# A scan and feed-forward kernel on one core: one of the four sums of g goes from the DMA queue to VectorE, with more descriptor scratch, a margin for late DMAs in the build-time order, and runs of 508 and 504 columns

## The chip, the cores and the metric

The kernel runs on one core of a Trainium2 chip. The metric is the device time of one execution in microseconds (us), the median of three runs; lower is better. One further execution was profiled, and every row of the trace below is from it.

## The reference

For two batches of 6080 tokens and 256 channels, a gated scan runs along the tokens, and its result, seen as 12160 rows, goes through two matrix products with a gate between them.

```python
f = lower_bound + (1 - lower_bound) * sigmoid(f_logit)
h = 0
for t in range(S):                      # S = 6080
    h = f[:, t] * h + (1 - f[:, t]) * x[:, t]
    y[:, t] = h
h = y.reshape(12160, 256) @ w_in        # 256 x 2048
g = h * clip(h + 3, 0, 6) / 6
out = g @ w_out                         # 2048 x 256
```

Everything is float32.

## The kernel before

**Runs.** Tokens lie along the free axis, channels on the 128 partitions. The tokens of both batches are cut into 24 runs of at most 512 columns (`token_runs`): 20 runs of 512 and 4 of 480. A product that must be float32-accurate is made of three matmuls, by splitting each operand into a high and a low part (`split`: a copy on ScalarE makes the high part, a subtraction on VectorE the low part).

**Products.** The first four runs multiply directly (`direct`, `single`, `mm2`). The other 20 runs go in ten pairs, one run of each batch, and their 2x2 block products are made with seven products in place of eight (`seven`), which needs sums of operands. For the first product these sums are made of the scan's result (`prep_pair`, tiles `xt`). For the second product of a pair, six of the sixteen blocks of 128 channels are treated so, in nine of the ten pairs (`chain`); the other ten blocks go directly (`mm2`).

**The chain.** `chain` works on four tiles of gated values, g11, g12, g21 and g22, in place: w11, w12, w21, w22. Each is there twice (index z): once for two blocks side by side, 1024 columns wide (names r4, r5, r6, r7 in the built program), once for one block, 512 wide (r10, r11, r12, r13). It makes seven operands, each split into high (`ghi`) and low (`glo`): b11 = w11; t1 = w11 += w12; t3 = w12 += w22; t2 = w11 += w22; b21 = w21; b22 = w22; t4 = w11 += w21. The four sums, for both z, are eight DMAs that add one SBUF tile to another, issued from GpSimd's queue (POOL, `add_into`, L250). TensorE takes the operands in the order b11, t1, t2, b21, b22, t3, t4, three blocks at a time, between other work.

**Order.** Every instruction is first a `Job` with an engine, a planned cost and the jobs that it needs. `ordered` gives each job a due time, plays the engines forward by the planned costs, and writes the program in that order. On the chip every engine then works strictly in its written order and waits by semaphores. So an instruction that waits holds up all that stand behind it on its engine.

**DMA scratch.** `SCRATCH = 512` is the number of bytes of each SBUF partition that hold the descriptors of DMAs issued from POOL. Loads of x and f and the stores of the output are issued from SP.

**Begin.** The first run is loaded and scanned in two halves. `SHARED` lists by (run, first column) the pieces whose second gate scaling (L377) is given to VectorE, not to ScalarE (L381); (0, 256) is the second half of run 0. While TensorE has nothing to do at the begin, it runs matmuls on zeros (L879), as many as the plan has room for.

Of the kernel before, what the change touches and what calls it, by code (L numbers as in the profile page):

```python
# [19 lines left out]
LAG = 4  # L20
PARTS = ((0, 1), (2,))
GROUP = sum(map(len, PARTS))
FILLS = ((2, 3, 2),) * 3 + ((2, 3, 3),)*5
FILLS_FIRST = ((2, 2, 2),) * 8

SHARED = ((0, 0), (0, 256), (1, 0))
# [81 lines left out]
HOP = {"PE": 230, "ACT": 70, "DVE": 70, "SP": 0, "POOL": 0}  # L108
ISSUE = 480
ISSUE_ADD = 1000  # L110
DIRECT = 4
FT = 1
EARLY_AT = {(2, 1): 7, (1, 0): 6, (2, 0): 5}
SCRATCH = 512
LANDING = 1700
SLOW_START = 6500
BYTES_PER_NS = 390
# [3 lines left out]
def ordered(jobs):  # L121


    for j in jobs:
        for b in j.bufs:
            if b.before is not None:
                j.needs.extend(u for u in b.before.users if u is not j)
    for j in jobs:
        j.needs = list(dict.fromkeys(j.needs))
        j.after = []  # L130
    for j in jobs:
        for n in j.needs:
            n.after.append(j)
    left = {j: len(j.after) for j in jobs}
    stack = [j for j in jobs if not left[j]]
    while stack:
        j = stack.pop()
        late = min((d.due for d in j.after), default=1e9) - HOP[j.engine] - j.cost
        if j.moves:
            late -= LANDING + j.moves / BYTES_PER_NS  # L140
        if j.at is None:
            j.due = late
        for n in j.needs:
            left[n] -= 1
            if not left[n]:
                stack.append(n)

    def early(j):
        return max(0.0, j.due - j.ahead) if j.due < 5e8 else 0.0
    missing = {j: len(j.needs) for j in jobs}  # L150
    ready = {e: [] for e in HOP}
    free = dict.fromkeys(ready, BEGIN)
    bus = 0.0
    number = {j: i for i, j in enumerate(jobs)}
    for j in jobs:
        if not missing[j]:
            ready[j.engine].append((early(j), j))
    order = []
    while any(ready.values()):
        best = None  # L160
        for e, waiting in ready.items():
            if waiting:
                start = max(free[e], min(r for r, _ in waiting))
                if best is None or start < best[0]:
                    best = (start, e)
        start, e = best
        could = [x for x in ready[e] if x[0] <= start]
        pick = min(could, key=lambda x: (x[1].due, number[x[1]]))
        ready[e].remove(pick)
        j = pick[1]  # L170
        j.start = start
        free[e] = end = start + j.cost
        if j.moves:
            bus = max(bus, end)
            slow = min(j.moves / 250, max(0, SLOW_START - bus))
            bus += slow + (j.moves - 250 * slow) / BYTES_PER_NS
            end = bus + LANDING
        j.end = end
        order.append(j)
        for d in j.after:  # L180
            missing[d] -= 1
            if not missing[d]:
                at = max(n.end + (HOP[n.engine] if n.engine != d.engine else 0) for n in d.needs)
                ready[d.engine].append((max(at, early(d)), d))
    assert len(order) == len(jobs)
    return order


def token_runs(B, S):


    runs = []
    full = (S - 1) // BANK - 1
    rest = S - full * BANK
    counts = [BANK] * full + [-(-rest // 2), rest // 2]
    assert counts[-1] == counts[-2] <= BANK
    s = 0
    for n in counts:
        runs.extend((b, s, n) for b in range(B))
        s += n  # L200
    return runs
# [3 lines left out]
def gated_scan_then_ffn(  # L205
# [42 lines left out]
    def add_into(size, out, src, needs, bufs):  # L248

        return job("POOL", ISSUE_ADD, lambda: nc.gpsimd.dma_start(out=out(), in_=src(), accum_op=ALU.add),  # L250
                   needs, bufs, moves=2 * size)

    r_ft = Ring(work, "ft", FT, [P, KD, BANK], F32)
    r_xt = Ring(work, "xt", 2, [P, KD, BANK], F32)
    r_xhi = Ring(work, "xhi", 4, [P, KD, BANK], F32R)
    r_xlo = Ring(work, "xlo", 4, [P, KD, BANK], F32R)
    r_bhi = Ring(work, "bhi", 1, [P, BANK], F32R)
    r_blo = Ring(work, "blo", 1, [P, BANK], F32R)
# [3 lines left out]
    r_ec = Ring(work, "ec", 1, [P, BANK], F32)  # L262
    r_e = Ring(work, "e", 2, [P, BANK], F32)
    r_ghi = Ring(work, "ghi", 4, [P, 2 * BANK], F32R)
    r_glo = Ring(work, "glo", 4, [P, 2 * BANK], F32R)
    banks = [Ring(psum, f"bank{k}_", 1, [P, BANK], F32) for k in range(8)]


# [172 lines left out]
    def prep_pair(h, h2):  # L441
# [201 lines left out]
    def seven(n, o, e, one, then, negative):  # L643


        o11, o12, o21 = o
        o22, e = e
        p1 = one(o21, "a11", "b11", [], True)
        s11 = copy(n, o11, o21, [p1], negative)
        yield  # L650
        p5 = one(o12, "s1", "t1", [], True)
        e_out = copy(n, e, o12, [p5], negative)
# [11 lines left out]
        s22 = add(n, o22, o21, e, [p7], negative)  # L664
        then(3, [s22])
        yield
        p4 = one(o21, "a22", "t4", [s22], False)
        then(2, [s22, p4])
# [3 lines left out]
    def quad(p, h, h2, group):  # L672
# [7 lines left out]
        if p < group:  # L680
            part = next(part for part in PARTS if p in part)
            if p == part[0]:
                raws.setdefault(h, []).append([r_r.at(4 + k) if len(part) == 2 else r_r1.at(k) for k in range(4)])
            outs = [(x, p - part[0]) for x in raws[h][-1]]
        else:
            x, y = r_r.at(2 * (p % 2)), r_r.at(2 * (p % 2) + 1)
            outs = [(x, 0), (y, 0), (y, 1), (x, 1)]

        def weight(name):
# [12 lines left out]

        def then(k, needs):
            done[k] = gate(n, (b, c, a, e)[k], needs, outs[k], k in (0, 3))
        yield from seven(n, (b, c, a), (e, e), one, then, True)
# [60 lines left out]
    def chain(h, h2):  # L766
# [20 lines left out]
        t3 = [[sum_into(w12[z], w22[z], [*g22[z], *t1[z]])] for z in every]  # L787
        t2 = [[sum_into(w11[z], w22[z], [*g22[z], *dt1[z]])] for z in every]
        dt2 = [operand("t2", w11, z, t2, True) for z in every]
        for z in every:  # L790
            operand("b21", w21, z, g21, False)
        for z in every:
            operand("b22", w22, z, g22, True)
        for z in every:
            operand("t3", w12, z, t3, True)
        t4 = [[sum_into(w11[z], w21[z], [*g21[z], *dt2[z]])] for z in every]
        for z in every:
            operand("t4", w11, z, t4, False)
# [21 lines left out]

        def step():
            if not steps:
                steps.append(seven(n, (o11, o12, o21), (o22, r_ec.new()), one, then, False))
            next(steps[0], None)
        queue.extend([(GROUP, step)] * 7)

# [85 lines left out]
```

## Time and profile before

| | |
|---|---|
| median of three runs | 1025.21 us (1022.83 to 1026.08) |
| profiled execution, its own time | 1024.29 us |
| its span, first to last instruction | 1022.5 us |
| TensorE busy | 995.7 us, 97% of the span |
| VectorE busy | 811.6 us, 79% |
| ScalarE busy | 704.7 us, 69% |
| GpSimd queue (POOL), busy with issuing | 98.2 us, 10% |

The profiled execution took 1.8 us more than its span, and stands 0.9 us below the median of the runs. Busy time of an engine says how long it worked, not what it waited for. TensorE's matmuls overlap in the pipeline, so its busy time hides part of its idle time, and counts of matmuls in a stretch tell more.

### The profile page before, as it was taken

How to read it: one execution, taken by the hardware profiler on the slowest of the kernel's cores; microseconds unless marked ns; L12 is line 12 of the kernel's file. 1: busy time of each engine (PE TensorE's matmuls, PEld its weight loads, DVE VectorE, ACT ScalarE, POOL GpSimd, SP SyncE). 2: the span in 40 equal slices, each digit the busy share in tenths (PEclk: the TensorE clock that was granted, in tenths of full speed). 3: DMA queues.
4: the chain of work that ended last, by engine and by line, in shares of the span. 5: the costliest groups of instructions: out<-in, count | busy, mean ns of one | idle time of the engine just before them, and what ended most of it. 6: DMA issues, size and time to landing. Idle time of an engine off the chain costs nothing.

```text
span 1022.5 us, 12064 instructions
## 1 busy us (share of the span) xinstructions
PE 995.7 (97%) x4315; PEld 803.8 (79%) x4316; DVE 811.6 (79%) x1114; ACT 704.7 (69%) x1150; POOL 98.2 (10%) x116
## 2 busy tenths in 40 slices
PE   9999999999999999999999999999999999899998
PEld 3788888888877887886887887788688688688787
DVE  7998898588659868867977985986896896697583
ACT  7976676586568677767767666866776776676662
POOL 0000001000120111111112012011111111101200
PEclk9999999999999999999999999999999999999999
DMA  8841032111262272244237127227225423612501
GB/s 329 287 165 41 22 103 63 60 44 21 42 175 52 42 184 52 53 126 102 52 67 169 32 52 180 47 42 185 54 50 125 98 49 70 150 35 49 126 10 39
DMA packets 42029, 93.19 MB, mean 91 GB/s; under 512 B 4080, under 2 KB 10736, under 8 KB 41968
## 3 DMA queue, kind: packets, MB, share of 16 engines
q0 software_dynamic: 16128, 38.28, 19.9%
q1 hardware_dynamic: 25424, 53.87, 15.5%
q8 instruction: 34, 0.56, 0.2%
q10 hardware_dynamic: 416, 0.26, 0.1%
q14 instruction: 27, 0.22, 0.1%
HBM read 41.67 MB, written 12.45 MB: 53 GB/s over the span
## 4 chain that ended last, share of the span: by engine, by line
PE 77%; issue 9%; DMA 5%; DVE 3%; ACT 3%; POOL 2%; POOLq 0%; ACTq 0%; DVEq 0%
PE bank L526 35%; PE bank L637 33%; PE bank L592 8%; DMA r<-r 5%; POOL r L250 2%; DVE glo L419 1%; ACT r L491 1%; ACT ghi L413 1%; PE bank L602 1%; DVE glo L422 1%; DVE e L626 1%; DVE bank L628 0%; DVE r L493 0%; ACT ec L618 0%; ACT r L567 0%
## 5 line engine op out<-in xcount | busy, mean ns | idle before, releaser
L491 ACT ACTIVATE r<-bank 128x512 f32<-128x512 f32 (+1 forms) x304 | 178.1, 591 | 120.0 <-PE bank L637 72.9
L493 DVE SCALAR_TENSOR_TENSOR r<-r,bank 128x512 f32<-128x512 f32 (+1 forms) x304 | 205.1, 677 | 59.2 <-ACT r L491 57.0
L637 PE MATMUL bank<-xhi,wst 128*128 128x512 f32 (+1 forms) x640 | 237.9, 392 | 11.3 <-DVE r L493 7.2
L526 PE MATMUL bank<-ghi,whi 128*128 128x512 f32 (+1 forms) x548 | 212.8, 388 | 0.0
L526 PE MATMUL bank<-glo,whi 128*128 128x512 f32 (+1 forms) x548 | 212.5, 388 | 0.0
L526 PE MATMUL bank<-ghi,wlo 128*128 128x512 f32 (+1 forms) x548 | 212.4, 388 | 0.0
L419 DVE SCALAR_TENSOR_TENSOR glo<-r,ghi 128x1024 fp32r<-128x1024 f32 (+3 forms) x125 | 131.0, 1054 | 44.0 <-ACT ghi L413 44.0
L637 PEld LDWEIGHTS bank<-xhi,wst 128*128 128x128 f32 x640 | 120.4, 188 | 43.4 <-DVE r L493 11.9
L422 DVE TENSOR_TENSOR glo<-r,ghi 128x1024 fp32r<-128x1024 f32 (+3 forms) x107 | 114.5, 1071 | 40.5 <-ACT ghi L415 40.4
L413 ACT ACTIVATE ghi<-r 128x1024 fp32r<-128x1024 f32 (+3 forms) x125 | 112.8, 920 | 47.3 <-DMA r<-r 34.9
L415 ACT CAST ghi<-r 128x1024 fp32r<-128x1024 f32 (+3 forms) x107 | 98.8, 928 | 40.5 <-DMA r<-r 22.5
L637 PE MATMUL bank<-xlo,wst 128*128 128x512 f32 (+1 forms) x320 | 124.1, 388 | 0.0
L526 PEld LDWEIGHTS bank<-ghi,wlo 128*128 128x128 f32 x548 | 102.9, 188 | 20.7 <-DVE wlo L299 0.2
L526 PEld LDWEIGHTS bank<-ghi,whi 128*128 128x128 f32 x548 | 102.9, 188 | 20.7 <-issue 0.2
L526 PEld LDWEIGHTS bank<-glo,whi 128*128 128x128 f32 x548 | 102.8, 188 | 20.7
L250 POOL DMA_DIRECT2D r<-r x72 | 62.9, 874 | 345.1 <-DVE r L493 154.3
L250 POOL DMA_DIRECT2D xt<-xt x40 | 35.1, 878 | 529.2 <-ACT r L491 178.6
L637 PE MATMUL bank<-ghi,whi 128*128 128x512 f32 (+1 forms) x180 | 70.8, 393 | 7.6 <-DVE bank L628 6.2
L637 PE MATMUL bank<-glo,whi 128*128 128x512 f32 (+1 forms) x180 | 70.9, 394 | 2.0 <-DVE glo L419 1.8
L628 DVE TENSOR_TENSOR bank<-bank,e 128x512 f32<-128x512 f32 (+1 forms) x80 | 55.0, 687 | 21.9 <-PE bank L637 18.8
L637 PE MATMUL bank<-ghi,wlo 128*128 128x512 f32 (+1 forms) x180 | 69.7, 387 | 0.0
L637 PEld LDWEIGHTS bank<-xlo,wst 128*128 128x128 f32 x320 | 60.4, 189 | 11.2
(104 smaller groups left out, 1486.4 us busy)
## 6 DMA issues: line engine op xcount, KB each, us to landing
r<-r POOLq DMA_DIRECT2D x28, 512.0 KB, 4.6
outT<-r SPq DMA_DIRECT2D x40, 256.0 KB, 2.9
xt<-xT SPq DMA_DIRECT2D x18, 512.0 KB, 5.0
ft<-fT SPq DMA_DIRECT2D x17, 512.0 KB, 3.9
xt<-xt POOLq DMA_DIRECT2D x32, 256.0 KB, 3.2
wst<-w SPq DMA_DIRECT2D x14, 512.0 KB, 4.1
r<-r POOLq DMA_DIRECT2D x28, 256.0 KB, 3.3
wst<-w SPq DMA_DIRECT2D x14, 511.5 KB, 4.9
```

The source lines that it names most:

```text
L250: return job("POOL", ISSUE_ADD, lambda: nc.gpsimd.dma_start(out=out(), in_=src(), accum_op=ALU.add), needs, bufs, moves=2 * size)
L413: nc.scalar.mul(to(hi), cut(src), -1.0)
L415: nc.scalar.copy(to(hi), cut(src))
L419: nc.vector.scalar_tensor_tensor(out=to(lo), in0=cut(src), scalar=-1.0, in1=to(hi).bitcast(F32), op0=ALU.mult, op1=ALU.subtract)
L422: nc.vector.tensor_tensor(to(lo), cut(src), to(hi).bitcast(F32), op=ALU.subtract)
L491: b = job("ACT", act_cost(n, psum=True), lambda: nc.scalar.activation(piece(r, i, n), src.get()[:, :n], AF.Relu, bias=3.0, scale=-1.0 if n ...
L493: return job("DVE", dve_cost(n), lambda: nc.vector.scalar_tensor_tensor(out=piece(r, i, n), in0=piece(r, i, n), scalar=6.0, in1=src.get()[ ...
L526: nc.tensor.matmul(bank.get()[:, :n], wt[f][:, D + m * P:D + (m + 1) * P], piece(g, half, n), start=(start and i == 0), stop=(stop and i = ...
L592: nc.tensor.matmul(ph.get()[:, o:e], wt[f][:, k * P:(k + 1) * P], x[h].get()[:, k, o:e], start=(i == 0), stop=(i == len(ops) - 1),)
L602: nc.tensor.matmul(ph.get()[:, o:e], cut(k), xt.get()[:, k, o:e], start=(k == 0), stop=(k == KD - 1))
L628: nc.vector.tensor_tensor(o, x, y, op=ALU.add)
L637: nc.tensor.matmul(bank.get()[:, :n], wt(), x(), start=(start and z == 0 and i == 0), stop=(z == len(parts) - 1 and i == 2), skip_group_ch ...
```

## The change

The sum t1 of the chain (both z) becomes an instruction on VectorE. t4 is made as w21 += w11, so that it needs t2 itself and no longer the split of t2; the like is done for the fourth sum of `prep_pair`. The scratch goes from 512 to 1024 bytes. In the plan a DMA of POOL lands `LATE` = 1500 ns later than it did, and is due so much earlier; t3 is planned not earlier than 8000 ns before it is due. The runs become 16 of 508 columns and 8 of 504. The list `FILLS` (how many pieces of second-product work go between the products of a pair) is changed in its order, with the same sum. `seven` is written twice, once for each of its two uses, with the same instructions.

```diff
-FILLS = ((2, 3, 2),) * 3 + ((2, 3, 3),)*5
+FILLS = ((2, 3, 2),) * 2 + ((2, 3, 3),) * 5 + ((2, 3, 2),)
...
+LATE = 1500
+ON_DVE = {("t1", 0), ("t1", 1)}
+AHEAD = 8000
...
-SCRATCH = 512
+SCRATCH = 1024
...
-            late -= LANDING + j.moves / BYTES_PER_NS
+            late -= LANDING + j.moves / BYTES_PER_NS + (LATE if j.engine == "POOL" else 0)
...
-            end = bus + LANDING
+            end = bus + LANDING + (LATE if j.engine == "POOL" else 0)
...
-    full = (S - 1) // BANK - 1
-    rest = S - full * BANK
-    counts = [BANK] * full + [-(-rest // 2), rest // 2]
+    count = -(-S // BANK)
+    base = S // count // 4 * 4
+    longer, rest = divmod(S - count * base, 4)
...
+        n = base + 4 * (i < longer)
...
-        j4 = sum_into(xt, 0, xt, 1, [*d2, *ss])
-        d4 = split(xt, *end, cut(0), n, j4, flip=True, to=whole)
+        j4 = sum_into(xt, 1, xt, 0, [*j2, *d_own])
+        d4 = split(xt, *end, cut(1), n, j4, flip=True, to=whole)
...
+        def sum_into(name, z, out, x, needs, ahead=None):
+            if (name, z) in ON_DVE:
+                return job("DVE", dve_cost(n * (out.shape[1] // BANK)), lambda: nc.vector.tensor_tensor(flat(out), flat(out), flat(x), op=ALU.add),
+                           needs, [out, x])
+            return add_into(4 * (out.shape[1] // BANK) * n * P, lambda: flat(out), lambda: flat(x), needs, [out, x], ahead)
...
-        t1 = [[sum_into(w11[z], w12[z], [*g12[z], *d11[z]])] for z in every]
+        t1 = [[sum_into("t1", z, w11[z], w12[z], [*g12[z], *d11[z]])] for z in every]
...
+        t3 = [[sum_into("t3", z, w12[z], w22[z], [*g22[z], *t1[z]], AHEAD)] for z in every]
+        t2 = [[sum_into("t2", z, w11[z], w22[z], [*g22[z], *dt1[z]])] for z in every]
...
-        t4 = [[sum_into(w11[z], w21[z], [*g21[z], *dt2[z]])] for z in every]
+        t4 = [[sum_into("t4", z, w21[z], w11[z], [*t2[z], *d21[z]])] for z in every]
```

On POOL, the second of the nine chains stood like this before. Each row is one DMA that adds the tile behind the arrow to the one ahead of it; in brackets are the semaphores that it waits for (DMASW: a landing of a POOL DMA, DVE: VectorE).

```order
L250 DMA r4_2918<-r5_2988 128x1024 [waits DMASW6_49,DVE_49]
L250 DMA r5_2988<-r7_3006 128x1024 [waits DMASW4_49,DVE_49]
L250 DMA r10_3068<-r11_3091 128x512 [waits DMASW7_49,DVE_49]
L250 DMA r11_3091<-r13_3109 128x512 [waits DMASW6_49,DVE_49]
L250 DMA r4_2918<-r7_3006 128x1024 [waits DVE_49]
L250 DMA r10_3068<-r13_3109 128x512 [waits DMASW1_49,DVE_49]
L250 DMA r4_2918<-r6_3018 128x1024 [waits DMASW0_49,DVE_49]
L250 DMA r10_3068<-r12_3128 128x512 [waits DMASW3_49,DMASW1_49,DVE_49]
```

The same chain on POOL with the change:

```order
L255 DMA r4_2932<-r7_3019 128x1016 [waits DMASW5_49,DMASW2_49,DVE_49]
L255 DMA r10_3069<-r13_3125 128x508 [waits DMASW3_49,DVE_49]
L255 DMA r5_3004<-r7_3019 128x1016 [waits DMASW4_49]
L255 DMA r11_3106<-r13_3125 128x508
L255 DMA r6_3029<-r4_2932 128x1016 [waits DMASW2_49,DVE_49]
L255 DMA r12_3151<-r10_3069 128x508 [waits DMASW7_49,DMASW3_49]
```

Two of eight rows are gone (t1), t3 has moved from the second and fourth place behind t2, and the last two write w21 (r6, r12).

At the begin of the program, ScalarE's rows from the second half of run 0 on, before and then with the change:

```order
L372 ACTIVATE ft0_106<-ft0_106 128x2x256
L381 ACTIVATE ft0_106<-ft0_106,gb_66,ga_65 128x256
L298 CAST whi0_69<-xhi2_110 128x256
L288 ACTIVATE xhi3_117<-xhi3_117 128x256
L290 ACTIVATE xhi3_117<-xhi3_117 128x256
L401 ACTIVATE last_67<-xt0_108 128x1
L372 ACTIVATE r6_121<-r6_121 128x1024
```

```order
L377 ACTIVATE ft0_106<-ft0_106 128x2x254
L386 ACTIVATE ft0_106<-ft0_106,gb_66,ga_65 128x254 x2
L293 ACTIVATE xhi3_117<-xhi3_117 128x256
L295 ACTIVATE xhi3_117<-xhi3_117 128x256
L303 CAST whi0_69<-xhi2_110 128x256
L377 ACTIVATE r6_121<-r6_121 128x2x508
L386 ACTIVATE r6_121<-r6_121,gb_66,ga_65 128x508
```

The gate scaling of the second half stands twice (x2): that half now begins at column 254, which `SHARED` does not list, so VectorE's part of it has come to ScalarE.

## Rows read from the trace of the kernel before

**Rows 1.** The page's busy times and share of the span.

```profile
PE 995.7 (97%) x4315; PEld 803.8 (79%) x4316; DVE 811.6 (79%) x1114; ACT 704.7 (69%) x1150; POOL 98.2 (10%) x116
```

**Rows 2.** Stretches: length, busy us (count) of PE, PEld, DVE, ACT, POOL; clock, DMA.

```profile
280.00:315.00 35.00, 32.32 (x137) 24.90 (x137) 23.34 (x31) 24.80 (x41) 6.11 (x7) 1.00 0.65 155
...
370.00:395.00 25.00, 23.39 (x98) 17.84 (x98) 17.25 (x23) 19.08 (x32) 5.25 (x6) 1.00 0.73 177
395.00:455.00 60.00, 60.00 (x266) 49.70 (x265) 50.50 (x65) 42.01 (x67) 6.11 (x7) 1.00 0.27 59
455.00:480.00 25.00, 23.05 (x97) 17.22 (x96) 18.08 (x24) 18.42 (x30) 4.39 (x5) 1.00 0.68 161
...
540.00:565.00 25.00, 23.64 (x100) 18.14 (x100) 19.78 (x26) 19.20 (x31) 4.35 (x5) 1.00 0.59 138
...
622.00:645.00 23.00, 20.68 (x86) 15.37 (x85) 16.46 (x21) 17.01 (x28) 4.37 (x5) 1.00 0.65 152
...
706.00:730.00 24.00, 21.93 (x91) 16.18 (x90) 17.51 (x24) 18.45 (x30) 4.38 (x5) 1.00 0.60 139
...
790.00:815.00 25.00, 22.64 (x96) 17.28 (x95) 19.22 (x26) 18.86 (x31) 4.38 (x5) 1.00 0.54 124
...
870.00:896.00 26.00, 22.29 (x93) 17.77 (x93) 16.94 (x24) 17.21 (x30) 4.37 (x5) 0.93 0.63 144
...
958.00:980.00 22.00, 19.11 (x82) 14.73 (x82) 15.01 (x22) 13.18 (x22) 3.48 (x4) 1.00 0.41 83
```

**Rows 3.** The chain of waits: pieces of matmuls at 512 and at 480 columns.

```profile
344.84 3.40 PE bank L526 x15
...
1003.26 15.59 PE bank L526 x72
```

**Rows 4.** Waits from 280 to 1000 us: who for whom, us, times, longest.

```profile
ACT ghi L413 <- DMA r<-r: 34.9, 18, 2.9
...
ACT ghi L415 <- DMA r<-r: 22.5, 12, 4.6
...
PE bank L637 <- DVE r L493: 7.2, 11, 2.2
...
PE bank L637 <- DVE bank L628: 6.8, 9, 0.8
...
PE bank L637 <- ACT bank L616: 3.4, 6, 1.1
```

**Rows 5.** POOL's timeline in the second chain: start, us, issue; idle before.

```profile
375.60 0.87 POOL L250 DMA_DIRECT2D r<-r  x1 [3.15 <-DVE glo L422]
379.27 0.88 POOL L250 DMA_DIRECT2D r<-r  x1 [2.80 <-issue]
384.80 0.87 POOL L250 DMA_DIRECT2D r<-r  x1 [4.66 <-DMA r<-r]
388.34 0.88 POOL L250 DMA_DIRECT2D r<-r  x1 [2.67 <-DMA r<-r]
```

**Rows 6.** The page's DMA queue of POOL, and its issues with us to landing.

```profile
q0 software_dynamic: 16128, 38.28, 19.9%
...
r<-r POOLq DMA_DIRECT2D x28, 512.0 KB, 4.6
...
r<-r POOLq DMA_DIRECT2D x28, 256.0 KB, 3.3
```

**Rows 7.** Groups by form: mean ns of the split on VectorE and ScalarE.

```profile
L422 DVE TENSOR_TENSOR glo<-r,ghi 128x1024 fp32r<-128x1024 f32 x64 | 77.8, 1216 | 10.7 <-ACT ghi L415 10.6
...
L422 DVE TENSOR_TENSOR glo<-r,ghi 128x512 fp32r<-128x512 f32 x21 | 14.4, 688 | 19.6 <-ACT ghi L415 19.6
...
L415 ACT CAST ghi<-r 128x1024 fp32r<-128x1024 f32 x64 | 66.9, 1046 | 9.3 <-PE bank L637 7.5 <-PE bank L526 1.6
```

**Rows 8.** Timeline of ScalarE and VectorE at the begin.

```profile
9.48 0.60 ACT L381 ACTIVATE ft<-ft,gb,ga 128x256 f32<-128x256 f32 x1
...
9.75 0.41 DVE L377 TENSOR_SCALAR ft<-ft,ga,gb 128x256 f32<-128x256 f32 x1
```

More of the change, by code (lines that the diff above doesn't have):

```diff
@@ L192, in token_runs @@
     runs = []
-    full = (S - 1) // BANK - 1
-    rest = S - full * BANK
-    counts = [BANK] * full + [-(-rest // 2), rest // 2]
-    assert counts[-1] == counts[-2] <= BANK
+    count = -(-S // BANK)
+    base = S // count // 4 * 4
+    longer, rest = divmod(S - count * base, 4)
+    assert not rest and base + 4 * (longer > 0) <= BANK
     s = 0
-    for n in counts:
+    for i in range(count):
+        n = base + 4 * (i < longer)
         runs.extend((b, s, n) for b in range(B))
@@ L218, in gated_scan_then_ffn @@
     runs = token_runs(B, S)
+    W = max(n for _, _, n in runs)
     assert B == 2 and KD == 2 and NF % 4 == 0 and len(runs) > 4 and len(runs) % 2 == 0
@@ L246, in load, with add_into @@
         return job(queue, ISSUE, lambda: engine.dma_start(out(), src), bufs=[buf] if buf else [], moves=size, ahead=EARLY)
-    def add_into(size, out, src, needs, bufs):
+    def add_into(size, out, src, needs, bufs, ahead=None):
         return job("POOL", ISSUE_ADD, lambda: nc.gpsimd.dma_start(out=out(), in_=src(), accum_op=ALU.add),
-                   needs, bufs, moves=2 * size)
-    r_ft = Ring(work, "ft", FT, [P, KD, BANK], F32)
-    r_xt = Ring(work, "xt", 2, [P, KD, BANK], F32)
+                   needs, bufs, moves=2 * size, ahead=ahead)
+    r_ft = Ring(work, "ft", FT, [P, KD, W], F32)
+    r_xt = Ring(work, "xt", 2, [P, KD, W], F32)
+    r_ec = Ring(work, "ec", 1, [P, W], F32)
     r_xhi = Ring(work, "xhi", 4, [P, KD, BANK], F32R)
     r_xlo = Ring(work, "xlo", 4, [P, KD, BANK], F32R)
-    r_bhi = Ring(work, "bhi", 1, [P, BANK], F32R)
-    r_blo = Ring(work, "blo", 1, [P, BANK], F32R)
+    r_bhi = Ring(work, "bhi", 1, [P, W], F32R)
+    r_blo = Ring(work, "blo", 1, [P, W], F32R)
     r_wst = Ring(work, "wst", 4, [P, 2, 2 * wide], U32)
@@ L261, in gated_scan_then_ffn @@
     r_r1 = Ring(work, "r1", 4, [P, BANK], F32)
[L262 to L265, printed above, removed]
+    r_e = Ring(work, "e", 2, [P, W], F32)
+    r_ghi = Ring(work, "ghi", 4, [P, 2 * W], F32R)
+    r_glo = Ring(work, "glo", 4, [P, 2 * W], F32R)
     banks = [Ring(psum, f"bank{k}_", 1, [P, BANK], F32) for k in range(8)]
@@ L641, in product, with seven, seven_in_banks @@
         return pe(n, 3 * len(parts), emit, [*before, *needs], [bank, *bufs])
-    def seven(n, o, e, one, then, negative):
-        o11, o12, o21 = o
-        o22, e = e
+    def seven(n, o, one, then):
+        o11, o12, o21, o22 = o
         p1 = one(o21, "a11", "b11", [], True)
-        s11 = copy(n, o11, o21, [p1], negative)
+        s11 = copy(n, o11, o21, [p1], True)
         yield
         p5 = one(o12, "s1", "t1", [], True)
-        e_out = copy(n, e, o12, [p5], negative)
+        e = copy(n, o22, o12, [p5], True)
+        yield
+        p6 = one(o21, "s2", "t2", [s11], False)
+        s12 = add(n, o12, o21, o22, [p6, e])
+        yield
+        p2 = one(o11, "a12", "b21", [s11], False)
+        then(0, [s11, p2])
+        yield
+        p3 = one(o12, "s4", "b22", [s12], False)
+        then(1, [s12, p3])
+        yield
+        p7 = one(o21, "s3", "t3", [s12], False)
+        s22 = add(n, o22, o21, o22, [p7], True)
+        then(3, [s22])
+        yield
+        p4 = one(o21, "a22", "t4", [s22], False)
+        then(2, [s22, p4])
+    def seven_in_banks(n, o, e, one, then):
+        o11, o12, o21, o22 = o
+        p1 = one(o21, "a11", "b11", [], True)
+        s11 = copy(n, o11, o21, [p1])
+        yield
+        p5 = one(o12, "s1", "t1", [], True)
+        e_out = copy(n, e, o12, [p5])
         yield
@@ L663, in seven @@
         p7 = one(o21, "s3", "t3", [s12], False)
-        s22 = add(n, o22, o21, e, [p7], negative)
+        s22 = add(n, o22, o21, e, [p7])
         then(3, [s22])
@@ L685, in quad @@
         else:
-            x, y = r_r.at(2 * (p % 2)), r_r.at(2 * (p % 2) + 1)
+            x, y = [r_r.at(2 * ((p - GROUP + 1) % 2) + k) for k in range(2)]
             outs = [(x, 0), (y, 0), (y, 1), (x, 1)]
@@ L704, in then @@
             done[k] = gate(n, (b, c, a, e)[k], needs, outs[k], k in (0, 3))
-        yield from seven(n, (b, c, a), (e, e), one, then, True)
+        yield from seven(n, (b, c, a, e), one, then)
         if p < group:
@@ L795, in chain @@
             operand("t3", w12, z, t3, True)
-        t4 = [[sum_into(w11[z], w21[z], [*g21[z], *dt2[z]])] for z in every]
         for z in every:
-            operand("t4", w11, z, t4, False)
+            operand("t4", w21, z, t4, False)
         def one(bank, wname, xname, needs, start):
@@ L822, in step @@
             if not steps:
-                steps.append(seven(n, (o11, o12, o21), (o22, r_ec.new()), one, then, False))
+                steps.append(seven_in_banks(n, (o11, o12, o21, o22), r_ec.new(), one, then))
             next(steps[0], None)
```

7 lines of the change are left out of this document (1 added, 6 removed).

## The prediction

> **What bounds the kernel now.** I read the page first: TensorE is busy 97% of the span, the next engine, VectorE, 79% [rows 1]. So the time is TensorE's, and a change can gain only where TensorE waits, or lose where it makes TensorE wait more. Busy time hides part of that, so I then took stretches and counted matmuls. From 395 to 455 us 266 matmuls run in 60.0 us, which is 266 × 0.2267 = 60.3: TensorE never stops there [rows 2]. The 0.2267 is 3.40 us for 15 matmuls of 512 columns; at 480 columns it is 15.59 / 72 = 0.2165 [rows 3]. The nine stretches around the nine chains are different. In the seven with 512 columns 137 + 98 + 97 + 100 + 86 + 91 + 96 = 705 matmuls take 182 us, and 705 × 0.2267 is 159.8: 22.2 us are lost. In the two with 480 columns 93 + 82 = 175 take 48 us against 37.9: 10.1 lost [rows 2]. **TensorE loses 32.3 us in the chains**, 2.3 to 5.9 in each. The granted clock is 1.00 in eight of them, so it is waiting and not a slow clock (0.93 in the one from 870, whose wait is the longest).
>
> The waits say who is late. TensorE waits for VectorE's gate (7.2 us), for VectorE's add into a bank (6.8) and for ScalarE's copy of a bank (3.4). None of these has to do with the sums; but ScalarE itself stands 34.9 + 22.5 = 57.4 us at the splits until a sum's DMA has landed [rows 4], and what stands behind the split on ScalarE (those copies and the first half of each gate) stands with it.
>
> Why the sums are late is in POOL's timeline. The issue at 384.80 was idle-ended by a landing, and the next one, at 388.34, comes 3.54 us later [rows 5], which is 3.3 us to landing [rows 6] and 0.3 more. The one at 379.27 came 3.67 us after the one at 375.60 with nothing in the profile that it waited for ("issue"), and again that is a landing and 0.3 [rows 5, 6]. I found no two issues of POOL closer than 3.5 us although issuing takes 0.87: the queue has one DMA in flight at a time. Eight sums of a chain, four of 4.6 us and four of 3.3, each with 0.3, are 32.8 us in a row [rows 6], and the chain can't be shorter.
>
> **The change part by part.** *t1 on VectorE, nine chains.* It removes two of the eight sums from POOL (4.9 + 3.6 = 8.5 us of the row of 32.8) and makes t1 ready when VectorE has added. No such add is in the trace; the nearest row is the subtraction with two SBUF inputs, 1.22 us at 1024 columns and 0.69 at 512 [rows 7], so 1.9 us a chain, 17 us in all on an engine that then works 811.6 + 17 = 829 us of about 993, 83% [rows 1]. Between two chains, 395 to 480 us, VectorE works 50.50 + 18.08 = 68.6 of 85 us [rows 2], and would work 70.5 of 82, 86%. In the 60 us in which it is at 84% now, TensorE does not wait [rows 2]. I cost it at nothing, hidden under matmuls; if that cover is gone it costs up to 17.
>
> *t4 into w21.* t4 can start when t2 has landed, without the split of t2 (1.05 us on ScalarE and 1.22 on VectorE, [rows 7]), 2.3 us sooner per chain. It is no path of its own; it counts in the margins below.
>
> *More scratch.* If the scratch is what holds the queue to one DMA, 1024 bytes let at least two be in flight, and the six sums that are left no longer stand in a row. Counted along the built program, the first matmul that reads a sum stands 49 to 109 matmuls (11.1 to 24.7 us at 0.2267) behind the matmul whose result starts it; before, the nearest was 40 (9.1 us), behind a queue. A wide sum needs split, landing and split, 2.3 + 4.6 + 2.3 = 9.2 us [rows 6, 7], and has 13.8 or more; a narrow one needs at most 2.3 + 3.3 + 2.3 = 7.9 and has 11.1 or more. Each has 3 us to spare, enough for the next issue (0.87) and for sharing the DMA engines with one other. Also the margins in the plan (LATE, AHEAD) only move rows, and put t3 behind t2 on POOL.
>
> So the 32.3 us should go. What is late next is VectorE, in order and dense: I leave a third of a us per chain, 3 us, between 0 (the stretch without waits) and 12.6 (the second case below). The sum: -29.3.
>
> *Runs of 508 and 504.* The columns and the matmuls stay as many. One clock column is 1 / 2.4 GHz, and 512 columns take 213.3 of the 226.7 ns, so 13.3 ns are on top; at 480 it is 216.5 - 200 = 16.5 [rows 3]. With 13.3 on top of each, 508 takes 225.0 and 504 223.3: per 24 runs 16 × 225.0 + 8 × 223.3 = 5387 against 20 × 226.7 + 4 × 216.5 = 5400, and at 4315 / 24 = 180 matmuls for a run [rows 1] that is -2.3 us. On the straight line between the two measured sizes it is 0. If anything below 512 is paced as 512, it is 24 × 226.7 = 5441, +7.4 us. I take -1. Their loads and stores are of as many bytes and lie under 60 us stretches in which the DMA share is 0.27 [rows 2].
>
> *The begin.* ScalarE gets a second gate scaling of 0.60 us in place of VectorE's of 0.41 that ran beside the first [rows 8]; the scan of that half starts some 0.5 us later. ScalarE's later rows shift with it. From -0.5 (filler work covers it) to +1.5 (three such steps): +0.5.
>
> *FILLS, seven, prep_pair's fourth sum:* same work in another order, around stretches without waits: 0.
>
> **Sum:** span 1022.5 - 29.3 - 1 + 0.5 = 992.7. The profiled execution took 1.8 more than its span and the median of the runs 0.9 more than that: **995.4 us**.
>
> **The rivals.** *VectorE's own pace.* The wait for its add into a bank comes nine times, once in each chain, with at most 0.8 us, whether the chain lost 2.3 or 5.9 [rows 2, 4]. That it is so even speaks for VectorE's own queue there, not for a late DMA. If so, its share of the three largest waits, 6.8 of 17.4, stays: 39% of 32.3 = 12.6 us. 1022.5 - 19.7 - 1 + 0.5 = 1002.3, so 1005. Against it: the row in front of that add on VectorE is a split that was held up.
>
> *Columns paced as 512.* The 480-column matmuls vary around their 216.5, and no run here has rows that begin at odd places; with +7.4 in place of -1 it is 1003.8.
>
> *One at a time all the same (slower).* If POOL keeps to one DMA for another reason than room, the next issue stays 0.3 us behind each landing. Six sums remain, 4.9 or 3.6 us each. In seven of nine chains the wide t4 stands last: 3.6 + 4.9 + 4.9 + 3.6 + 3.6 us of others, then 4.6, lands 25.2 us after the first issue. ScalarE comes to its split 84 matmuls, 19.0 us, after the matmul that starts the first, and the first issue is 1.5 us behind that: it stands 25.2 + 1.5 - 19.0 = 7.7 us. In the other two chains t4 has two fewer behind it and I get 5.9. Together 66 us, against 57.4 now, which cost TensorE 32.3, 0.56 each: 36.9, so +4.6. 1022.5 + 4.6 - 1 + 0.5 = 1026.6, so 1029: slower. It decides where two issues of POOL come no closer than a landing.
>
> The page "DMA: Bandwidth & Descriptors" of the Trainium skill speaks for this rival: its section "The descriptor swizzle" gives 9 read and 9 write descriptors per engine for a transfer over 128 partitions, and its "Terms" 16 bytes for a descriptor. The trace agrees with the nine: 16128 packets of 112 issues on 16 engines [rows 6]. By an estimate from that page 512 bytes hold 32 descriptors, three such DMAs, so room would not be what holds the queue to one, and the time would be that of this rival, 1029; by the rows alone (one at a time, whatever the size) it is open how much an adding DMA takes.
>
> **How the numbers follow.** Forecast 0.62, with its own range 990 to 1002 (nothing left of the waits, or 9 us of them, with the bounds of columns and begin); VectorE's pace 0.17 (1001 to 1010); columns 0.08 (1000 to 1008); one at a time 0.10 (1024 to 1035); 0.03 for mixtures near no change. Below 989 I leave 0.04, above 1009 about 0.15: 989 to 1009. About 0.3%, 3.1 us, is what can be told from no change. Faster, below 1022.1: 0.62 + 0.17 + 0.08 and some of the mixtures, 0.88; within 0.04; slower 0.08.
>
> **What would show it.** Right: in POOL's timeline issues 0.9 to 1.5 us apart within a chain; ScalarE's wait for sums below 15 us in all; the chains' stretches with 0.2250 us for a matmul throughout. t1: adds of 1.2 and 0.7 us on VectorE and no wait behind them. Columns: back-to-back matmuls at 225.0 and 223.3 ns. Begin: dense matmuls from about 24.5 us on, not 24. Wrong: issues still 3.5 us apart (one at a time), a wait for the add into a bank in each chain (VectorE), 226.7 ns for 508 columns.

## The result and the profile after

The changed kernel takes **1007.74 us** (median of four runs, 1007.38 to 1008.19) against 1024.47 us before (four runs): a ratio of 0.9837, 95% interval 0.9819 to 0.9855, 16.7 us less. The forecast was 995.4 us with a range of 989 to 1009. The direction and the range held; only 56% of the forecast gain (16.7 of 29.8 us) came.

The page of the kernel after gives busy time and share of each engine, and its DMA issues (KB each, us to landing):

```profile
PE 998.9 (99%) x4318; PEld 807.5 (80%) x4319; DVE 827.4 (82%) x1131; ACT 708.1 (70%) x1151; POOL 82.1 (8%) x98
...
r<-r POOLq DMA_DIRECT2D x15, 508.0 KB, 6.6
```

TensorE was at 97% and is at 99% [rows 1], and yet some 13 us of the forecast gain did not come (the span is 1006.2 us, forecast 992.7). The stretches say where. Columns as in [rows 2]:

```profile
280.00:315.00 35.00, 34.84 (x152) 28.18 (x151) 27.05 (x37) 26.91 (x45) 5.22 (x6) 1.00 0.59 142
...
370.00:395.00 25.00, 25.00 (x110) 20.44 (x109) 21.76 (x30) 21.01 (x35) 5.26 (x6) 1.00 0.80 188
395.00:455.00 60.00, 60.00 (x262) 49.05 (x262) 49.49 (x64) 40.77 (x65) 3.47 (x4) 1.00 0.22 52
455.00:480.00 25.00, 25.00 (x110) 20.40 (x110) 20.79 (x29) 20.76 (x32) 5.27 (x6) 1.00 0.64 138
```

The stretches around the chains are full: 110 matmuls in the 25 us from 370, where it was 98 [rows 2]. But the stretch without waits, 395 to 455, holds 262 matmuls where it held 266, though each has fewer columns. So the chains gave back what they lost, and every matmul became longer. The chain of waits (start, us, engine, tile, line, matmuls) gives the length:

```profile
374.29 27.62 PE bank L642 x120
...
986.77 15.76 PE bank L531 x69
```

27.62 / 120 is 230.2 ns for 508 columns and 15.76 / 69 is 228.4 ns for 504; 512 columns took 226.7 before [rows 3]. As means over all records, the starts follow each other by 229.7 ns (508) and 228.4 ns (504).

The waits from 280 to 1000 us (who for whom, us, times, longest) show that the chains themselves are cured:

```profile
ACT ghi L418 <- DMA r<-r: 2.4, 4, 1.0
...
PE bank L642 <- DVE bank L633: 0.2, 1, 0.2
PE bank L642 <- ACT bank L621: 0.2, 1, 0.2
```

ScalarE stood 57.4 us for the sums [rows 4], now 2.4; the add into a bank, for which TensorE waited nine times, is waited for once, 0.2 us. POOL's timeline of the second chain:

```profile
375.26 0.89 POOL L255 DMA_DIRECT2D r<-r  x1 [26.42 <-DVE glo L427]
376.76 1.76 POOL L255 DMA_DIRECT2D r<-r  x2 [0.62 <-DVE glo L427]
381.68 0.86 POOL L255 DMA_DIRECT2D r<-r  x1 [3.16 <-DMA r<-r]
384.42 0.89 POOL L255 DMA_DIRECT2D r<-r  x1 [1.88 <-DVE glo L427]
387.58 0.87 POOL L255 DMA_DIRECT2D r<-r  x1 [2.27 <-DVE glo L424]
```

Issues 1.5 and 0.9 us apart where none was closer than 3.5 [rows 5]: several sums are in flight, and each takes longer to land (6.6 us for a wide one, 4.6 before [rows 6]). The groups by form show t1 on VectorE, 1.21 us wide and 0.68 narrow as the subtractions of [rows 7], with next to no idle time before it:

```profile
L804 DVE TENSOR_TENSOR r<-r,r 128x1016 f32<-128x1016 f32 x5 | 6.0, 1208 | 0.0
...
L804 DVE TENSOR_TENSOR r<-r,r 128x508 f32<-128x508 f32 x5 | 3.4, 681 | 0.1
```

At the begin, ScalarE's timeline has the two gate scalings in a row where VectorE had one of them [rows 8]; TensorE is not later for it: the matmul that started at 34.12 us starts at 34.00. The two scalings:

```profile
9.41 1.09 ACT L386 ACTIVATE ft<-ft,gb,ga 128x254 f32<-128x254 f32 x2
```

### The profile page after: what moved, and what is told of

It reads as the page before. It is cut to its first block, busy times and chain, and to the rows that moved or that the text cites. A ratio compares the mean times of both kernels' runs of the same rounds, so it can differ in the third digit from the quotient of the medians.

```text
span 1006.2 us, 11995 instructions
## 1 busy us (share of the span) xinstructions
PE 998.9 (99%) x4318; PEld 807.5 (80%) x4319; DVE 827.4 (82%) x1131; ACT 708.1 (70%) x1151; POOL 82.1 (8%) x98
## 4 chain that ended last, share of the span: by engine, by line
PE 96%; DMA 1%; ACT 1%; DVE 1%; issue 0%; ACTq 0%; DVEq 0%
PE bank L642 50%; PE bank L531 37%; PE bank L597 8%; DMA r<-r 1%; PE bank L607 1%; DMA xt<-xT 0%; PE bank L528 0%; DVE xt L389 0%; DVE xt L399 0%; ACT ghi L420 0%; ACT xhi L420 0%; ACT r L377 0%; ACT xhi L295 0%; ACT r L386 0%; ACT xhi L293 0%
## 5 line engine op out<-in xcount | busy, mean ns | idle before, releaser
L496 ACT ACTIVATE r<-bank 128x508 f32<-128x508 f32 (+1 forms) x304 | 179.6, 593 | 125.8 <-PE bank L642 87.7
L498 DVE SCALAR_TENSOR_TENSOR r<-r,bank 128x508 f32<-128x508 f32 (+1 forms) x304 | 204.3, 676 | 65.7 <-ACT r L496 64.8
L642 PE MATMUL bank<-xhi,wst 128*128 128x508 f32 (+1 forms) x640 | 234.2, 392 | 0.2 <-ACT bank L621 0.2
L531 PE MATMUL bank<-ghi,whi 128*128 128x508 f32 (+1 forms) x548 | 215.1, 393 | 0.0
L531 PE MATMUL bank<-glo,whi 128*128 128x508 f32 (+1 forms) x548 | 214.6, 392 | 0.0
L531 PE MATMUL bank<-ghi,wlo 128*128 128x508 f32 (+1 forms) x548 | 214.5, 391 | 0.0
L424 DVE SCALAR_TENSOR_TENSOR glo<-r,ghi 128x1016 fp32r<-128x1016 f32 (+3 forms) x125 | 130.4, 1053 | 15.2 <-ACT ghi L418 15.2
L418 ACT ACTIVATE ghi<-r 128x1016 fp32r<-128x1016 f32 (+3 forms) x125 | 114.7, 925 | 27.5 <-PE bank L642 14.6
L427 DVE TENSOR_TENSOR glo<-r,ghi 128x1016 fp32r<-128x1016 f32 (+3 forms) x107 | 114.8, 1074 | 16.5 <-ACT ghi L420 15.5
L642 PE MATMUL bank<-xlo,wst 128*128 128x508 f32 (+1 forms) x320 | 125.2, 391 | 0.0
L642 PE MATMUL bank<-ghi,whi 128*128 128x508 f32 (+1 forms) x180 | 70.5, 392 | 0.2 <-DVE bank L633 0.2
L642 PE MATMUL bank<-glo,whi 128*128 128x508 f32 (+1 forms) x180 | 70.5, 392 | 0.0
L642 PE MATMUL bank<-ghi,wlo 128*128 128x508 f32 (+1 forms) x180 | 70.4, 391 | 0.0
```

Source lines behind the costliest of these rows:

```text
L418: nc.scalar.mul(to(hi), cut(src), -1.0)
L424: nc.vector.scalar_tensor_tensor(out=to(lo), in0=cut(src), scalar=-1.0, in1=to(hi).bitcast(F32), op0=ALU.mult, op1=ALU.subtract)
L427: nc.vector.tensor_tensor(to(lo), cut(src), to(hi).bitcast(F32), op=ALU.subtract)
L496: b = job("ACT", act_cost(n, psum=True), lambda: nc.scalar.activation(piece(r, i, n), src.get()[:, :n], AF.Relu, bias=3.0, scale=-1.0 if n ...
L498: return job("DVE", dve_cost(n), lambda: nc.vector.scalar_tensor_tensor(out=piece(r, i, n), in0=piece(r, i, n), scalar=6.0, in1=src.get()[ ...
L531: nc.tensor.matmul(bank.get()[:, :n], wt[f][:, D + m * P:D + (m + 1) * P], piece(g, half, n), start=(start and i == 0), stop=(stop and i = ...
```

## The experiments

Theory: the scratch ended the waits of the chains, and runs of 508 and 504 columns cost about 17 us of it. Rivals: the matmuls are longer because the engines now crowd each other ("crowding"), or t1 off the queue is what helped ("t1"). Each kernel was timed in five rounds beside the kernel before on the same chip, unless said otherwise; times are medians. A label after_512_... means after_runs512 (the first experiment) with the edit shown on top of it; those programs were timed on other chips than after_runs512, each beside the kernel before.

### The runs of before in the changed kernel

```diff
-SCRATCH = 1024
+SCRATCH = 704
...
-    count = -(-S // BANK)
-    base = S // count // 4 * 4
-    longer, rest = divmod(S - count * base, 4)
...
+    full = (S - 1) // BANK - 1
+    rest = S - full * BANK
+    counts = [BANK] * full + [-(-rest // 2), rest // 2]
...
```

> The changed kernel with the runs of before (20 of 512, 4 of 480 columns), and 704 bytes of scratch in place of 1024, since 512 columns leave no room for more. Theory 'columns': each matmul of 508 or 504 columns takes longer than one of 512 (229.7 and 228.4 ns by start-to-start distances in the trace after), 17 us over the program, so this kernel takes 1007.7 - 17 = 991 us, and its matmuls follow each other at 226.7 ns. Rival 'crowding': the spacing grew because VectorE, ScalarE and the DMAs now overlap more with TensorE's reads; then 512 columns too take some 229 ns here and the time stays near 1007. Rival 'room': with less scratch only one DMA fits again and the chains wait, 1020 or more.

Measured: 993.28 us against 1025.12, ratio 0.9691 (0.9674 to 0.9708). The stretches:

```profile
370.00:395.00 25.00, 25.00 (x112) 20.69 (x111) 21.96 (x30) 21.07 (x32) 5.25 (x6) 1.00 0.71 161
395.00:455.00 60.00, 60.00 (x267) 49.67 (x266) 51.16 (x66) 42.78 (x70) 5.93 (x7) 1.00 0.28 69
```

TensorE has no gap in the chain either, and 512 columns are at 226.6 ns again, by the records, with all the other work as dense. "Crowding" falls. Everything in the change but the runs and what follows from them (the width of the tiles, and with it the room for 1024 bytes) is worth 31.8 us (1025.12 - 993.28); the runs cost 1007.74 - 993.28 = 14.5 us of it.

The matmuls themselves became longer by more than that. Taken from the records (for each size the count times the mean distance of starts, with distances of 260 ns and more left out of the mean), they sum to 989.3 us in the changed kernel and to 970.6 here: 18.7 us. What the long distances hold above the mean, between 35 and 980 us, is TensorE's waiting: 1.0 us in the changed kernel and 5.2 here. So 4.2 us came back, because longer matmuls leave the sums more time: 18.7 - 4.2 = 14.5.

### The new runs in the kernel before

```diff
-    full = (S - 1) // BANK - 1
-    rest = S - full * BANK
-    counts = [BANK] * full + [-(-rest // 2), rest // 2]
+    count = -(-S // BANK)
+    base = S // count // 4 * 4
+    longer, rest = divmod(S - count * base, 4)
...
```

> The kernel before with the runs of 508 and 504 columns and nothing else of the change. Theory 'columns': +17 us of spacing, of which a few us fall into the waits of the nine chains, 1036 to 1042 us. Rival 'crowding': no change, 1023 to 1027.

Measured: 1037.71 us against 1025.12, ratio 1.0133 (1.0112 to 1.0153), 12.6 us slower. The cost is the runs' own, with and without the rest.

### Matmuls by themselves

```diff
+SECTIONS = ((512, 512, 0), (508, 512, 0), (504, 512, 0), (500, 512, 0), (496, 512, 0), (480, 512, 0), (448, 512, 0), (384, 512, 0),
+            (508, 508, 0), (512, 512, 4), (508, 512, 4))
...
+                    nc.tensor.matmul(bank[:, :n], wt[:, i * P:(i + 1) * P], xhi[:, at:at + n], start=(i == 0), stop=(i == 2))
```

> Matmuls by themselves, on zeros, 72 of each size in groups of three into one bank, with nothing of the reference computed: 512, 508, 504, 500, 496, 480, 448, 384 columns with rows that begin at multiples of 512 columns, then 508 with rows at multiples of 508, and 512 and 508 with rows that begin 4 columns later; first with the other engines idle, then with ScalarE and VectorE running 1024-column copies. Theory 'columns': 512 at 226.7 ns, 508 and 504 at 228 to 230, in both halves. Rival 'begin of rows': 508 at 225.0 where rows begin at multiples of 512, and over 228 at 508 or 4 columns later. Rival 'crowding': 225.0 and 223.3 while the other engines are idle, more while they run.

Measured, one execution, mean distance from the start of one matmul's record to the next, in ns (72 of each; `begin` is where rows begin, in columns; the last column is the prediction's 13.3 ns, 32 / 2.4, on top of the columns):

```
columns, begin     others idle   others busy   (columns + 32) / 2.4
512, 0 or 512          226.7         226.7         226.7
508, 0 or 512          227.6         227.6         225.0
504, 0 or 512          227.0         227.0         223.3
500, 0 or 512          223.4         223.4         221.7
496, 0 or 512          223.3         223.3         220.0
480, 0 or 512          216.7         216.7         213.3
448, 0 or 512          202.7         202.6         200.0
508, 0 or 508          228.9         228.9         225.0
512, 4 or 516          231.7           -           226.7
508, 4 or 516          226.7           -           225.0
```

In the second half the copies on VectorE and ScalarE ended at about 361.7 and 359.9 us. The last two sizes ran from 353 us on, most of it behind that end, so there is no value for them with the others busy. The groups by form of the second half agree (busy of 72 matmuls; the last one's end adds 0.16 us to the busy time of a group: 16.34 / 72 is 226.9 ns for 504):

```profile
L46 PE MATMUL bank<-xhi,wt 128*128 128x504 f32 x72 | 16.5, 388 | 0.0
L46 PE MATMUL bank<-xhi,wt 128*128 128x496 f32 x72 | 16.2, 385 | 0.0
L46 PE MATMUL bank<-xhi,wt 128*128 128x500 f32 x72 | 16.2, 385 | 0.0
L46 PE MATMUL bank<-xhi,wt 128*128 128x480 f32 x72 | 15.8, 378 | 0.0
```

For the eight rows that have both values, VectorE and ScalarE running beside it change nothing. 508 and 504 columns cost as much as 512 or a little more (the theory had said 228 to 230), and a row that begins 4 columns later costs 512 columns 5 ns (508 columns, which then end where 512 would, nothing). By number alone, 24 runs take 16 x 227.6 + 8 x 227.0 = 5458 ns against 20 x 226.7 + 4 x 216.7 = 5401: 57 ns, and at 180 matmuls for a run 10.2 us by an estimate from these matmuls.

### The new runs with tiles that begin as for 512

```diff
-    W = max(n for _, _, n in runs)
+    W = BANK
...
-SCRATCH = 1024
+SCRATCH = 704
```

> The changed kernel with its runs of 508 and 504 columns, but with every tile as wide as for 512 (W = BANK), so that all tiles begin at multiples of 64 bytes, as in before_runs508; 704 bytes of scratch, which is what then fits. The second halves of wide tiles still begin 508 or 504 columns in. Theory 'begin of rows': part of the longer spacing comes from where rows begin; the mean goes from 229.4 to the 228.4 ns of before_runs508, 4 us less: 1002.5 to 1005. Rival 'number of columns alone': 1006.5 to 1008.5.

Measured: 1003.96 us against 1025.50, ratio 0.9790 (0.9773 to 0.9807): 3.8 us less than the change. In the chain of waits the same piece as above is shorter:

```profile
371.37 27.44 PE bank L642 x120
```

27.44 / 120 is 228.7 ns, not 230.2. W is a part of the change that the list ahead of the prediction does not name: the changed kernel makes most of its tiles only as wide as its longest run, 508 columns, where the kernel before has 512. With W = 508 the built program places its tiles at multiples of 32 bytes, with W = 512 at multiples of 64. By the records, as above, the matmuls of this run sum to 985.0 us. So of the 18.7 us by which they became longer, 14.4 go with the number of columns, more than the 10.2 us by themselves, and 4.3 with where the tiles begin. The scratch, which also differs here, is not what did it: in before_runs508, with 512 bytes of scratch and tiles at multiples of 64, the mean distances are 228.1 ns (508) and 228.8 (504), here 228.1 and 228.7.

### More scratch alone

```diff
-SCRATCH = 512
+SCRATCH = 640
```

> The kernel before with 640 bytes of scratch in place of 512 and nothing else (eight sums on the queue, runs of 512 and 480). Theory 'room': two DMAs are in flight, issues come 0.9 us apart, and most of the 32 us of waits in the chains goes: 993 to 1003 us. Rival 't1': the chain needs t1 off the queue, since eight sums of 4.6 to 6 us still follow each other at two at a time: 1008 to 1020. Rival 'one at a time': 1024.

Measured: 997.13 us against 1025.12, ratio 0.9728 (0.9711 to 0.9744). One number gives 28.0 of the 31.8 us. POOL's timeline and the waits from 280 to 1000 us:

```profile
371.85 1.78 POOL L250 DMA_DIRECT2D r<-r  x2 [5.66 <-DVE glo L422]
375.70 0.89 POOL L250 DMA_DIRECT2D r<-r  x1 [2.06 <-issue]
```

```profile
ACT ghi L413 <- DMA r<-r: 14.8, 16, 1.4
...
ACT ghi L415 <- DMA r<-r: 10.8, 9, 1.4
...
PE bank L637 <- DVE bank L628: 3.0, 7, 0.8
```

Two issues follow each other at once, as the theory "room" said, and the time is in its range. ScalarE still stands 25.6 us for sums, and the add into a bank is still waited for in seven chains.

### The change with the old scratch, and with 576 bytes

```diff
-SCRATCH = 704
+SCRATCH = 512
```

> As after_runs512 (everything of the change but the runs, which are 512 and 480), with 512 bytes of scratch in place of 704. Theory 'room': one DMA in flight again, issues 0.3 us behind each landing; by the working of the rival in the prediction the first half of the chain's last split waits longer than before, and the time is 1020 to 1032. Rival 't1 and plan': the six sums left fit in a row since t1 is off the queue, 995 to 1010.

Measured: 1055.73 us against 1024.72, ratio 1.0301 (1.0288 to 1.0314), 31 us slower than before and 62 us slower than with 704 bytes, on the same program order but for that number. Both stated ranges (1020 to 1032, and 995 to 1010) missed it. POOL's timeline and the waits:

```profile
392.71 0.87 POOL L254 DMA_DIRECT2D r<-r  x1 [3.84 <-DVE r L497]
396.26 0.89 POOL L254 DMA_DIRECT2D r<-r  x1 [2.67 <-issue]
399.80 0.87 POOL L254 DMA_DIRECT2D r<-r  x1 [2.65 <-issue]
```

```profile
ACT ghi L419 <- DMA r<-r: 35.9, 8, 9.2
ACT ghi L417 <- DMA r<-r: 28.4, 11, 4.5
PE bank L641 <- DVE bank L632: 27.6, 9, 4.7
```

Issues are 3.5 us apart again. Not all of the 62 us is waiting. The clock that TensorE was granted is 0.982 over the span, where it is 1.000 in after_runs512: seven times it fell to its lower level, 1.2 GHz, where TensorE had stood. One such stretch, behind a wait of 4.7 us (length, busy us and count of PE, clock, DMA):

```profile
core 0: 1054.0 us, clock 0.982
...
407.00:413.40 6.40, 5.51 (x13) 0.50 0.00 1
```

In these stretches 61 matmuls follow each other at 423 ns on average and not at 226.7, which is 12 us of the 62. Which of the other edits makes the chains need the room more than in the kernel before was not tried.

```diff
-SCRATCH = 704
+SCRATCH = 576
```

> As after_runs512 with 576 bytes of scratch in place of 704. Theory 'descriptors': a sum takes 18 entries of 16 bytes (9 to read, 9 to write), so 576 bytes hold 36, two sums, like 704 (44): 992 to 995, issues 0.9 us apart in twos. Rival 'bytes in powers of two' or a spare entry in the ring: 576 holds only one, as 512 does, and the time is that of after_512_scratch512.

Measured: 993.72 us against 1024.72, ratio 0.9698 (0.9685 to 0.9710), as with 704. Its timeline has two issues 1.25 us apart:

```profile
382.94 0.87 POOL L254 DMA_DIRECT2D r<-r  x1 [2.24 <-issue]
384.19 0.88 POOL L254 DMA_DIRECT2D r<-r  x1 [0.38 <-DVE r L497]
```

So 512 bytes hold one sum and 576 hold two: if every sum takes the same and nothing else stands there, one takes more than 256 and at most 288 bytes. The three issues within 2.4 us in the changed kernel, with 1024 bytes, fit that.

### t1 alone on VectorE, and t1 left on the queue

```diff
-        t1 = [[sum_into(w11[z], w12[z], [*g12[z], *d11[z]])] for z in every]
+        t1 = [[job("DVE", dve_cost(n * (w11[z].shape[1] // BANK)), lambda z=z: nc.vector.tensor_tensor(
+            flat(w11[z]), flat(w11[z]), flat(w12[z]), op=ALU.add), [*g12[z], *d11[z]], [w11[z], w12[z]])] for z in every]
```

> The kernel before with t1 alone on VectorE (512 bytes of scratch, runs of 512 and 480, the other edits not made). Theory 'room': with one DMA in flight six sums still stand in a row of 25 us, less than the eight of 33 us, so only a part of the 32 us comes back: 1010 to 1022. Rival 't1': the queue was too long by these two, and the waits go: 993 to 1003. Rival 'no help': 1024 to 1030.

Measured: 1027.81 us against 1024.72, ratio 1.0032 (1.0019 to 1.0044). Neither theory's number: with two sums fewer on the queue the kernel is 3 us slower. The waits:

```profile
ACT ghi L413 <- DMA r<-r: 43.1, 18, 4.4
...
PE bank L637 <- ACT bank L616: 18.8, 7, 3.6
```

ScalarE stands less in all (43.1 + 1.6 against 57.4 [rows 4]) but at other splits, those in front of its copies of a bank, and TensorE waits for these 18.8 us where it was 3.4. Part of the 3 us is again the clock:

```profile
core 0: 1025.5 us, clock 0.991
```

It is 0.998 in the kernel before. By the records 31 matmuls at the lower level cost 6.1 us here, and six cost 1.0 us in the kernel before. Without these 5 us t1 alone would be some 2 us faster and not 3 slower, by an estimate from these two executions: six sums in place of eight hardly shorten the waits. In the changed order t1 was left on the queue:

```diff
-ON_DVE = {("t1", 0), ("t1", 1)}
+ON_DVE = set()
```

> As after_runs512 (704 bytes) with t1 left on POOL's queue: eight sums a chain, two in flight, the plan's margins and t4 into w21 as in the change. Theory 'room': t1 on VectorE matters little once two DMAs fit; the time is that of before_scratch640 or a little less, 994 to 998. Rival 't1': without it the chain waits again by 0.5 to 1 us at several places in each chain, 999 to 1010.

Measured: 996.21 us against 1024.72, ratio 0.9723 (0.9711 to 0.9736): t1 on VectorE is worth 2.9 us, once there is room and margin.

### Without the margins of the plan

```diff
-LATE = 1500
+LATE = 0
...
-AHEAD = 8000
+AHEAD = 1e9
```

> As after_runs512 without the margins of the plan (LATE = 0, t3 planned as early as it can). The prediction costs the margins at nothing: 992.5 to 994.5. Rival 'plan': they keep ScalarE from standing at the splits, and without them the waits of before_scratch640 (25.6 us of ScalarE, 3.8 of TensorE) come back: 996 to 1000.

Measured: 1002.51 us against 1025.50, ratio 0.9774 (0.9755 to 0.9792): 9.2 us more than with the margins, beyond the rival's range, and 5.4 more than the scratch alone: without the margins the other edits cost more than they bring. The waits from 280 to 1000 us, and ScalarE's timeline in the second chain:

```profile
ACT ghi L417 <- DMA r<-r: 20.2, 12, 2.8
...
PE bank L641 <- ACT bank L620: 8.2, 6, 2.1
```

```profile
375.31 0.60 ACT L495 ACTIVATE r<-bank 128x512 f32<-128x512 f32 x1
378.12 0.63 ACT L417 ACTIVATE ghi<-r 128x512 fp32r<-128x512 f32 x1 [2.21 <-DMA r<-r]
...
381.06 0.57 ACT L620 ACTIVATE bank<-bank 128x512 f32<-128x512 f32 x1
```

ScalarE stands 2.2 us at the split of the narrow t2, and the copy of a bank, for which TensorE waits, is four rows behind it (TensorE waits 8.2 us in all for such copies, 1.7 in after_runs512). Was it t3 in front of t2 on POOL?

```diff
-AHEAD = 8000
+AHEAD = 1e9
```

> As after_runs512 with the margin for late DMAs kept (LATE = 1500) and only the planned distance of t3 taken away, so that in the chain t3's two sums stand ahead of t2's on POOL, as in after_512_no_margin. Theory 't3 in front of t2': ScalarE's wait of after_512_no_margin is for t2, whose DMA stands behind t3's, which nobody needs yet; the time stays at 1000 to 1004. Rival 'LATE': the margin alone moves t2's split back far enough, 992.5 to 995.

Measured: 993.09 us against 1023.89, ratio 0.9698 (0.9684 to 0.9713). t3 stands first on POOL in both, so its place alone does not cost the 9.2 us, and LATE alone is enough to avoid them. Counted along the two built programs, from the narrow t2 on POOL to its split on ScalarE, 38 to 42 matmuls stand between in four of the nine chains and 26 to 32 in the others; without LATE it is 24 to 32 in all nine. With both margins (after_runs512) it is 24 to 30 in seven chains, and there t2 stands ahead of t3. AHEAD alone, without LATE, was not run, so whether t2's place would have been enough as well stays open.

### Runs of 512 and 448

```diff
-    full = (S - 1) // BANK - 1
-    rest = S - full * BANK
-    counts = [BANK] * full + [-(-rest // 2), rest // 2]
...
+    full = S // BANK
+    counts = [BANK] * full + [S - full * BANK]
...
```

> As after_runs512 (704 bytes of scratch) with 22 runs of 512 columns and two of 448 in place of 20 of 512 and four of 480. From the spacing of matmuls by themselves (512: 226.7, 480: 216.7, 448: 202.7 ns): 22 x 226.7 + 2 x 202.7 = 5393 against 20 x 226.7 + 4 x 216.7 = 5401 ns for each of 180 matmuls of a run, 1.4 us less than 993.3: 991.0 to 992.7. Rival: the last pair's chain gets less cover under shorter matmuls and gives it back, 993 to 995.

Measured: 991.77 us against 1025.50, ratio 0.9672 (0.9655 to 0.9689), the fastest version, 16.0 us below the changed kernel. Its interval overlaps that of after_runs512 (0.9674 to 0.9708), so the 1.5 us between the two are not clear of noise. The number came, the reason only in part: 448 columns took 206.0 ns in this program, not 202.7, which leaves 0.3 of the 1.4 us; the rest is in what TensorE waits between 840 and 880 us (2.1 us in after_runs512, 0.6 here).

## Why the prediction was half right

The time came to lie in the stated range, 989 to 1009, but not in the forecast's own, 990 to 1002. The range had been drawn wide for the rivals, and one of them came. So the number held by luck as far as one term of the sum, the runs, goes; the others are near.

*What bounds the kernel* was right: 32.3 us stood in the chains behind sums that came one at a time, and all but about 1 us of it is gone in the kernel after (all but 5 with runs of 512 columns, where the sums have less time). The row of eight sums is 34.0 us, four times 4.9 and four times 3.6, and not 32.8; nothing else rests on it.

*More scratch* was right, and carries nearly all: 28.0 us alone and 31.8 with the other edits, against the 29.3 forecast for the chains. The rival "one at a time all the same" fell with POOL's timeline. The section "The descriptor swizzle" of the page "DMA: Bandwidth & Descriptors" of the Trainium skill need not speak for that rival: it gives 9 read and 9 write descriptors for each engine, and the prediction counted only nine against the scratch. If all eighteen take from the same bytes, they are 288 bytes at the 16 of its section "Terms", by an estimate from that page, so that 512 hold one and 576 hold two; the traces agree, with one and two sums in flight at 512 and 576 bytes. With nine, 144 bytes by the same estimate, 512 would hold three, and the traces do not agree. How the descriptors lie in the scratch no run shows.

That rival's mechanism was nevertheless sound where the room is missing: it put ScalarE's stand at 66 us, and after_512_scratch512 shows 35.9 + 28.4 = 64.3 (at two kinds of split, where the rival had it all at the last one, so that the nearness is in part luck). Its price for TensorE was too low: 0.56 us for each, from [rows 4], where TensorE lost about 62 us against after_runs512 there. Of these, 12 are matmuls at the lower clock, for which the rival had no term.

*t1 on VectorE at no cost, as part of what empties the queue*: no cost was right (the adds have no idle time before them and nobody waits). The benefit is small: 2.9 us in the changed order, and with the old scratch 3 us lost, the lower clock included.

*The margins "only move rows": 0* was wrong. They are worth 9.2 us: a DMA that lands later than planned stops ScalarE, which works in order, and a plan without that knowledge puts the bank copies behind it. In the chain shown, the narrow t2 was issued at 370.07 us and its split began at 378.12, 8 us later, where the plan without LATE allows 4.0 (1.0 to issue, 1.3 to move, 1.7 to land). The counts of 49 to 109 matmuls of cover, on which the forecast rested, were those of a program made with the margins.

*What is late next: VectorE, 3 us* was too much: 0.2 us in the kernel after. The rival "VectorE's own pace" saw something real: with the scratch alone its add is still waited for in seven chains. The other edits together remove it; they are worth 3.8 us over the scratch alone (997.13 - 993.28). Of these, t4 into w21, the order of `FILLS`, the fourth sum of `prep_pair` and another choice of `r` tiles, which the list ahead of the prediction does not name, were not run by themselves.

*The begin: +0.5* did not come: the same matmul starts 0.12 us earlier.

**Runs of 508 and 504: -1 us** is the step that failed. It measured +14.5 us. The prediction took a value between two readings of [rows 3], a constant 13.3 ns on top of the columns (-2.3 us) and the straight line through 512 and 480 columns (0). Both suppose that 508 columns take less than 512, and no row had a size between. It gave the rival "columns paced as 512" (+7.4 us) a chance of 0.08. That rival was the right mechanism and itself too low: by themselves the two sizes take 0.9 and 0.3 ns more than 512, in after_bases512 1.4 and 2.0, in the changed kernel 3.0 and 1.7. The records make that 14.4 us for the number of columns and 4.3 for the packing of the tiles, which the prediction did not consider, less the 4.2 that TensorE then waits less. With these the sum reads 1024.5 - 31.8 + 14.4 + 4.3 - 4.2 = 1007.2, against 1007.74.

Still open is why 508 columns take as long as 512, why they take longer in a program than by themselves, and why in the changed kernel matmuls of 508 columns whose rows happen to begin at a multiple of 64 bytes take 229.8 ns, as long as the others.

## What to carry to other kernels

Before moving work off a queue that issues one DMA at a time, look whether it lacks room for a second: here 64 more bytes of scratch (512 to 576, in the changed order) were worth 62 us, more than every other edit, and without them the other edits made it slower. Where TensorE stands longer, look at its granted clock too before all of the loss is put down to waiting. A plan for engines that work in order has to assume DMAs as late as the trace shows them, since a wait costs what stands behind it. Take the time of a matmul of another size from a measurement at that size and at that place in memory; fewer columns can take longer.

## What the runs showed of the hardware that was not expected

A float32-rounded matmul of 500 and of 496 columns takes nearly the same, 223.4 and 223.3 ns, and 504 and 508 take 227.0 and 227.6, more than 512 with 226.7. 512 columns whose rows begin 4 columns late take 231.7. Copies of 1024 columns on VectorE and ScalarE beside it change none of the values up to 512 columns; the rows that begin late were taken without them. In a program it is not one value but a spread: 213 and 221 ns alternate at 480 columns, and 448 columns took 202.7 ns by themselves and 206.0 in the kernel.
